# A second batch in mixed precision forms, and a planner with other costs

## The chip, the cores and the metric

The kernel runs on one core of a Trainium2 chip. The metric is the device time of one execution in microseconds (us). The programs of a core's engines run side by side and wait for each other by semaphores: TensorE (PE) multiplies matrices, VectorE (DVE) and ScalarE (ACT) work element by element, GpSimd (POOL) does the same kind of work, and SyncE (SP) issues all DMA transfers from one queue. Each engine takes its instructions strictly in the order of its program.

## The reference, cut to what matters

```
batch, n_heads, seq, head_dim = 4, 12, 448, 64
scores = where(causal, q @ k.T / sqrt(64), -1e9)       # per head, 448 x 448
attn   = softmax(scores)
x      = (attn @ v) -> 1792 tokens x 768               # heads side by side
g, val = x @ w_gate, x @ w_val                         # 768 -> 1536
out    = (g * sigmoid(g) * val) @ w_out                # 1536 -> 768
```

The weights arrive as 64-bit floats. All results have float32 precision.

## The kernel before, in words

**Tiling.** The four batches are four chunks of 448 tokens. For each chunk come the attention of 12 heads in pairs (heads 0 and 1, 2 and 3, ...) and then the gated layer ("MoE" in the code), which is computed transposed: 12 blocks of 128 hidden columns, each with a gate and a value product, then six output blocks. Attention of chunk c+1 is worked in between the matmuls of chunk c's gated layer.

**Two forms of a product.** TensorE takes a float32 product either in float32 itself, which costs four passes over the columns, or in the reduced format `float32r` with one pass. The gated layer splits each operand into a high part and a low part (`x = xh + xl`, `w = wh + wl`) and adds three one-pass products: lines 667, 668 and 669. Heads of a pair marked `'s'` (split) do the same: scores from `QS` and `KS` (line 431, three passes), values from `ph`, `pl` and `VS` (lines 551 and 553), where `VS` holds the high and the low part of V side by side, and the upper and lower halves of the result are added afterwards (`tmp`, line 561, and `xs`, line 562). Splitting costs element-wise work: `QS`, `KS` and `VS` twice each, `ph` and `pl` for each group of key blocks. Heads marked `'n'` multiply float32 directly: scores from `qraw` and `kraw`, values from `ph` and `vraw` (line 581). There each head has 64 rows or 64 columns of the array, so that the two heads of a pair share it; their values are multiplied for both heads in one step, and one copy (line 588) brings the pair's result to `xs`. Which form a pair takes is told by two lists, `NS` for the scores and `NP` for the values, with one entry a batch, read by `nat` (line 48): letter number `(h // 2) % len(entry)` holds for head `h`. Before, all pairs of batch 0 are `'n'` and all others `'s'`.

**The steps of a head.** Scores into PSUM (`S`); row maximum with the mask (line 453, VectorE); exponential (line 462, ScalarE); reciprocal of the sums (lines 473 and 474, VectorE); normalisation (lines 483, 487, 491, one of three engines); transposes by TensorE into `T` (line 512); copies `ph` of the transposed blocks (line 522), for split heads low parts (line 535); values into `O`; result to `xs`, split into `xh` and `xl` for the gated layer (lines 599 and 600). For split heads the first key block of 64 rows carries its high and low parts in one tile, so the VectorE operation for its low part writes `ph` as well (profile rows `ph<-T,ph`).

**The weights.** There are 36 groups of 128 x 768. In chunk 0 each is loaded as 64-bit pairs (`wide`), converted by one scaling and three bit operations on VectorE (`wraw`, lines 637, 641, 645), split into `whl` (lines 656 and 657) and stored in DRAM (`ws`, line 658). The later chunks load `ws` (line 622). So VectorE's weight work lies wholly in chunk 0.

**The order.** The order of all instructions is worked out before the run by `Planner.run` (line 93). Every operation has a due time, dependences, buffers that it takes, and for each engine that may do it a cost (`cost`, line 53). The planner goes through a modelled time: the engine takes, among the ready operations that can start at about the same moment, the one that is due first; where several engines may do an operation, the one that would end it first. `lock` models that GpSimd and some VectorE operations (`port`) exclude one another. The costs are nowhere used on the chip; they only set the order and which engine does what. On TensorE a change of kind (`t` for transposes against all other) adds `TURN`, a score step `TS`, a float32 value step `TV`.

Of the kernel before, what the change touches and what calls it, by code (L numbers as in the profile page):

```python
# [23 lines left out]
XD = [-10.0, 3.0]  # L24
CS = 0.0
UW = 0
NS = ['n', 's', 's', 's']
NP = ['n', 's', 's', 's']
LEN = [46.6, 112.0, 258.9, 133.6, 58.1]
FRAC = 0.96  # L30
FRAC0 = 0.6
# [3 lines left out]
BIAS = {'DVE': 1.3, 'ACT': 0.8, 'POOL': 0.8}  # L35
PVLATE = 0
LAT = {"PE": 0.29, "DVE": 0.2, "ACT": 0.23, "POOL": 0.2, "SP": 0.1}
TURN = 0.088
TS = 0.38
SG = [[[3, 0]], [[2, 1]]]  # L40
TV = 0.1
WINDOW = 96
KBUS = 1 / 320
DLAT = 1.8
# [38 lines left out]
class Planner:  # L83
# [9 lines left out]
    def run(self, caps):  # L93
        free = dict.fromkeys(("PE", "DVE", "ACT", "POOL", "SP"), 0.0)
        ring = {}
        lock = {"DVE": 0.0, "POOL": 0.0}
        wire = 0.0
        kind = None

        def begin(o, e, t):  # L100
            if e == "POOL":
                return max(t, lock["DVE"])
            if e == "DVE" and o.port:
                return max(t, lock["POOL"])
            return t

        def slots(tag):
            if tag not in ring:
                c = caps.get(tag.rstrip("0123456789"), 1)
                ring[tag] = [None] * c  # L110
            return ring[tag]

        avail = {e: [] for e in free}

        def push(o):
            for e in o.alts:
                avail[e].append(o)
            dirty.update(o.alts)

        def ready(o, e):  # L120
            t = 0.0
            for d in o.deps:
                x = d.end if d in o.soft else d.end + d.extra + (LAT[d.eng] if d.eng != e else (0.0 if e == "PE" else 0.13))
                if x > t:
                    t = x
            for i, r in enumerate(o.alloc):
                h = slots(r.tag)[sum(x.tag == r.tag for x in o.alloc[:i])]
                if h is not None:
                    if h.left:
                        return None  # L130
                    if h.end > t:
                        t = h.end
            return t

        def finish(o, e, s):
            best = s + o.alts[e][0] + BIAS.get(e, 0.0)
            for f in o.alts:
                if f != e:
                    r = ready(o, f)
                    if r is not None and begin(o, f, max(r, free[f])) + o.alts[f][0] + BIAS.get(f, 0.0) + 1e-6 < best:  # L140
                        return False
            return True

        def choose(e):
            lst = avail[e]
            lst.sort(key=lambda o: (o.due, o.idx))
            cand = []
            for o in lst[:WINDOW]:
                r = ready(o, e)
                if r is not None:  # L150
                    s = begin(o, e, max(r, free[e]))
                    if len(o.alts) == 1 or finish(o, e, s):
                        cand.append((s, o))
            if not cand:
                return None
            lim = max(min(s for s, _ in cand), free[e]) + DELTA[e]
            if e == "PE" and kind == "t":
                for s, o in cand:
                    if s <= lim and o.kind == "t":
                        return s, o  # L160
            for s, o in cand:
                if s <= lim:
                    return s, o
            return None

        dirty = set(free)
        for o in self.ops:
            if o.nd == 0:
                push(o)
        order = []  # L170
        left = len(self.ops)
        while left:
            best = None
            for e in free:
                c = choose(e)
                if c is not None and (best is None or (c[0], c[1].due) < (best[0], best[1].due)):
                    best = (c[0], c[1], e)
            assert best is not None
            s, o, e = best
            for f in o.alts:  # L180
                avail[f].remove(o)
            o.start, o.eng = s, e
            o.end = s + o.alts[e][0]
            if e == "PE":
                o.end += TURN * (o.kind == "t" != kind)
                kind = o.kind
            o.fn = o.alts[e][1]
            free[e] = o.end
            if e == "SP":
                wire = max(wire, o.end) + o.kb * KBUS  # L190
                o.extra = wire + DLAT - o.end
            if e == "POOL" or (e == "DVE" and o.port):
                lock[e] = o.end
            for r in o.alloc:
                q = slots(r.tag)
                q.pop(0)
                q.append(r)
            for r in o.uses:
                r.left -= 1
                r.end = max(r.end, o.end + o.extra + LAT[e])  # L200
            for d in o.outs:
                d.nd -= 1
                if d.nd == 0:
                    push(d)
            order.append(o)
            left -= 1
        return order
# [7 lines left out]
def kernel(  # L215
# [86 lines left out]
    def binary(n, out, a, b, alu=ALU.subtract, engines="DP", kind="two"):  # L302
        r = {}
        if "D" in engines:
            r["DVE"] = (cost("DVE", "two", n), lambda: nc.vector.tensor_tensor(out(), a(), b(), alu))  # L305
        if "P" in engines:
            r["port"] = True
            r["POOL"] = (cost("POOL", kind, n), lambda: nc.gpsimd.tensor_tensor(out(), a(), b(), alu))
        return r
# [294 lines left out]

    seq = [(c, g) for c in range(NCHUNK) for g in range(NW)]
    scratch = [dpool.tile([P, 2, WC], F32, tag=f"ws{g}", name=f"ws{g}") for g in range(NW)]
    wt, wops, stored = {}, {}, {}

    def weights(i):
        c, g = seq[i]  # L610
        due = start[c + 1] + LEN[c + 1] * g / NW
        w = wt[i] = {}
        rhl = Res("whl")

        def newhl():
            w["hl"] = buf([P, 2, WC], F32R, "whl", "whl", f"whl{i}")
            w["h"], w["l"] = w["hl"][:, 0], w["hl"][:, 1]

        if c:
            def load():  # L620
                newhl()
                nc.sync.dma_start(raw(w["hl"]), scratch[g])
            ld = op({"SP": (0.3, load), "kb": 768}, due - 10 * WLEAD, [stored[g]], [rhl])
            wops[i] = (ld, ld, rhl, rhl)
            return
        rw, r64 = Res("wraw"), Res("wide")

        def load():
            w["wide"] = buf([P, WC, 2], U32, "wide", "wide", f"wide{i}")
            nc.sync.dma_start(w["wide"], wP[g].bitcast(U32).rearrange("p (n w) -> p n w", w=2))  # L630
        ld = op({"SP": (0.3, load), "kb": 768}, due - 16 * WLEAD, alloc=[r64])
        hi = lambda: w["wide"][:, :, 1]
        hf = lambda: w["wide"].bitcast(F32)[:, :, 1]

        def shift():
            w["raw"] = buf([P, WC], F32, "wraw", "wraw", f"wraw{i}")
            nc.vector.tensor_scalar(w["raw"].bitcast(U32), hi(), 3, None, ALU.logical_shift_left)  # L637

        def sign():
            a = w["raw"].bitcast(U32)  # L640
            nc.vector.scalar_tensor_tensor(a, hi(), 0x80000000, a, ALU.bitwise_and, ALU.bitwise_or)  # L641

        def low():
            a = w["raw"].bitcast(U32)
            nc.vector.scalar_tensor_tensor(a, w["wide"][:, :, 0], 29, a, ALU.logical_shift_right, ALU.bitwise_or)  # L645

        dv = lambda kind, f: {"DVE": (cost("DVE", kind, WC), f), "port": True}
        g0 = op(copies("sbuf", WC, hf, hf, 2.0**-112), due - 10 * WLEAD, [ld], [], [r64])
        d0 = op(dv("one", shift), due - 9.5 * WLEAD, [g0], [rw], [r64])
        d1 = op(dv("two", sign), due - 9 * WLEAD, [d0], [], [r64, rw])  # L650
        ra = op(dv("two", low), due - 8.5 * WLEAD, [d1], [], [r64, rw])

        def newh():
            newhl()
            return w["h"]
        h = op(copies("sbuf", WC, newh, lambda: w["raw"]), due - 6 * WLEAD, [ra], [rhl], [rw])
        l = op(binary(WC, lambda: w["l"], lambda: w["raw"], lambda: raw(w["h"])), due - 5 * WLEAD, [h], [], [rw, rhl])
        stored[g] = op({"SP": (0.3, lambda: nc.sync.dma_start(scratch[g], raw(w["hl"]))), "kb": 768}, due - 3 * WLEAD,
                       [h, l], [], [rhl])
        wops[i] = (h, l, rhl, rhl)  # L660

    ps = {}

# [141 lines left out]
```

## Time and profile before

| | |
|---|---|
| median of three runs | 732.53 us (731.42 to 734.65) |
| the profiled execution, its span | 734.49 us, 732.7 us |
| busy: PE, DVE, ACT, POOL | 712.6, 395.5, 352.7, 220.8 us |
| instructions: PE, DVE, ACT, POOL | 3948, 921, 898, 256 |
| mean granted clock of TensorE | 0.991 |
| chain that ended last | PE 76%, DVE 14%, ACT 5%, DMA 3% |

Busy time counts the time in which an engine has at least one instruction running. In the rows below, PE is a matmul and PEld the load of its stationary operand. A float32 matmul has two records each. Times count from the first instruction of the profiled execution. A row that ends in brackets tells how long the engine was idle before it, and which engine's operation ended that.

### The profile page before, as it was taken

The numbers are of one execution on the slowest core, as the hardware profiler recorded it, in microseconds if no ns is written. First come the engines' busy times: TensorE is split into PE (matmuls) and PEld (weight loads), VectorE is DVE, ScalarE is ACT, GpSimd is POOL, SyncE is SP. The second block draws the span as 40 slices with busy tenths as digits, with TensorE's granted clock in tenths as the row PEclk, the third lists the DMA queues.
The fourth block names the chain that finished last, engine by engine and source line by source line (L and its number), as shares of the span: only waits on it lengthen the run. The fifth ranks groups of instructions, "written<-read, shape, count | busy, mean of one in ns | idle before, by whom it ended". The sixth has DMA issues, their size and how long they took to land.

```text
span 732.7 us, 10983 instructions
## 1 busy us (share of the span) xinstructions
PE 712.6 (97%) x3948; PEld 615.5 (84%) x3948; DVE 395.5 (54%) x921; ACT 352.7 (48%) x898; POOL 220.8 (30%) x256
## 2 busy tenths in 40 slices
PE   7999998999989999999999999999999999999997
PEld 3556987887878898898888988888888899999997
DVE  5888998999999455444453244554462222222100
ACT  6899466866847445345355253453462421111100
POOL 3686537564556142134222121231330000000000
PEclk9899999999999999999999999999999999999999
DMA  8787885887997865455565665644545566666671
GB/s 297 234 286 268 292 317 189 299 306 271 313 335 276 314 238 195 162 197 195 189 216 192 213 209 184 212 172 134 178 164 197 178 217 216 216 215 216 213 255 39
DMA packets 39798, 165.08 MB, mean 225 GB/s; under 512 B 4416, under 2 KB 13632, under 8 KB 39744
## 3 DMA queue, kind: packets, MB, share of 16 engines
q1 hardware_dynamic: 39744, 164.38, 64.3%
q8 instruction: 31, 0.51, 0.3%
q14 instruction: 23, 0.19, 0.1%
HBM read 130.55 MB, written 33.82 MB: 224 GB/s over the span
## 4 chain that ended last, share of the span: by engine, by line
PE 76%; DVE 14%; ACT 5%; DMA 3%; issue 1%; SPq 0%; ACTq 0%; DVEq 0%
PE M L667 13%; PE M L669 13%; PE M L668 13%; PE MO L667 7%; PE MO L669 7%; PE MO L668 7%; PE T L512 6%; PE S L431 5%; PE O L551 3%; DVE wraw L641 3%; DVE wraw L645 3%; DVE wraw L637 2%; ACT p L462 2%; PE O L553 2%; DVE whl L305 2%; DMA wide<-in_w_dram 2%
## 5 line engine op out<-in xcount | busy, mean ns | idle before, releaser
L667 PE MATMUL M<-xh,whl 128*128 128x448 f32 x576 | 217.1, 377 | 0.2 <-DVE t L703 0.2
L669 PE MATMUL M<-xh,whl 128*128 128x448 f32 x576 | 210.7, 366 | 0.0
L668 PE MATMUL M<-xl,whl 128*128 128x448 f32 x576 | 210.5, 365 | 0.0
L667 PEld LDWEIGHTS M<-xh,whl 128*128 128x128 f32 x576 | 108.3, 188 | 10.5 <-DVE t L703 0.5
L669 PEld LDWEIGHTS M<-xh,whl 128*128 128x128 f32 x576 | 108.2, 188 | 9.1
L668 PEld LDWEIGHTS M<-xl,whl 128*128 128x128 f32 x576 | 108.4, 188 | 8.1
L462 ACT ACTIVATE p<-p,m 64x64 f32<-64x64 f32 (+3 forms) x192 | 96.2, 506 | 37.9 <-DVE m L453 36.2
L667 PE MATMUL MO<-hh,whl 128*128 128x448 f32 x288 | 108.3, 376 | 0.0
L669 PE MATMUL MO<-hh,whl 128*128 128x448 f32 x288 | 105.8, 367 | 0.0
L668 PE MATMUL MO<-hl,whl 128*128 128x448 f32 x288 | 105.5, 366 | 0.0
L453 DVE CUSTOM_DVE_ANT_0 p<-S,mask 64x64 f32<-64x64 f32 (+1 forms) x192 | 70.6, 414 | 48.4 <-PE S L431 46.0
L283 ACT ACTIVATE ph<-T 64x448 fp32r<-64x448 f32 (+1 forms) x144 | 64.0, 503 | 44.3 <-PE T L512 42.8
L512 PE MATMUL T<-ident,p 128*128 128x128 f32 (+2 forms) x480 | 69.1, 280 | 1.2 <-POOL p L487 0.5
L512 PEld LDWEIGHTS T<-ident,p 128*128 128x128 f32 (+2 forms) x480 | 51.8, 132 | 21.3 <-issue 7.7
L703 DVE SCALAR_TENSOR_TENSOR t<-t,M 128x448 f32<-128x448 f32 x48 | 29.6, 617 | 64.5 <-ACT t L699 64.3
L283 ACT ACTIVATE hh<-t 128x448 fp32r<-128x448 f32 x38 | 21.9, 576 | 82.9 <-DVE t L709 82.9
L487 POOL TENSOR_SCALAR p<-p,rec 128x320 f32<-128x320 f32 (+3 forms) x77 | 45.0, 595 | 49.5 <-ACT p L462 30.1
L667 PEld LDWEIGHTS MO<-hh,whl 128*128 128x128 f32 x288 | 54.4, 189 | 4.7
L669 PEld LDWEIGHTS MO<-hh,whl 128*128 128x128 f32 x288 | 54.3, 189 | 4.7
L668 PEld LDWEIGHTS MO<-hl,whl 128*128 128x128 f32 x288 | 54.5, 189 | 4.2
L709 DVE TENSOR_TENSOR t<-t,M 128x448 f32<-128x448 f32 x48 | 29.6, 617 | 50.0 <-PE M L669 49.7
L699 ACT ACTIVATE t<-M 128x448 f32<-128x448 f32 x48 | 26.0, 542 | 59.9 <-PE M L669 58.4
(59 smaller groups left out, 911.1 us busy)
## 6 DMA issues: line engine op xcount, KB each, us to landing
whl<-ws SPq DMA_DIRECT2D x108, 768.0 KB, 4.3
wide<-in_w_dram SPq DMA_DIRECT2D x36, 768.0 KB, 6.0
ws<-whl SPq DMA_DIRECT2D x36, 768.0 KB, 4.5
vraw<-in_v_dram SPq DMA_DIRECT2D x24, 256.0 KB, 4.7
qraw<-in_q_dram SPq DMA_DIRECT2D x24, 224.0 KB, 4.0
kraw<-in_k_dram SPq DMA_DIRECT2D x24, 224.0 KB, 4.1
out_dram<-osb SPq DMA_DIRECT2D x24, 224.0 KB, 4.7
```

Source lines behind the costliest of these rows:

```text
L283: nc.scalar.activation(out(), in_(), AF.Copy, scale=scale)
L431: nc.tensor.matmul(st[u + y][f"S{i}"][: q1_ - q0], Q[:, q0:q1_], K[:, :q1_], start=z == 0, stop=z == len(passes) - 1)
L453: nc.vector.tensor_tensor_reduce(p[:r], s[f"S{i}"][:r], mask[:r, maskX - q0 : maskX - q0 + q1_], -0.125, 3.0e38, ALU.add, ALU.min, m[:r],)
L462: nc.scalar.activation(p[:r], p[:r], AF.Exp, bias=s[f"m{i}"][:r], scale=-1.0, accum_out=sums[u % NR][:r, i : i + 1],)
L487: nc.gpsimd.tensor_scalar(p[:r], p[:r], rec[u % NR][:r, i : i + 1], 0.0, ALU.mult, ALU.add)
L512: nc.tensor.transpose(pt[:kn, o_ + q0 - bs : o_ + q1_ - bs], s[f"p{i}"][:r, U.kb[j][0] : U.kb[j][1]], ident[:r, :r])
L667: nc.tensor.matmul(out[:, :n], a[:, w], xhi, start=first, stop=False)
L668: nc.tensor.matmul(out[:, :n], a[:, w], xlo, start=False, stop=False)
L669: nc.tensor.matmul(out[:, :n], l[:, w], xhi, start=False, stop=last)
L699: nc.scalar.activation(t, ps[c, f, 0][:, :N], AF.Tanh, scale=0.5)
L703: nc.vector.scalar_tensor_tensor(t, t, 1.0, ps[c, f, 0][:, :N], ALU.add, ALU.mult)
L709: nc.vector.tensor_tensor(t, t, ps[c, f, 1][:, :N], ALU.mult)
```

## The change

Batch 1's entry in both lists becomes `'ns'`: its pairs 0, 2 and 4 (heads 0, 1, 4, 5, 8, 9) take the float32 form, pairs 1, 3 and 5 stay split. The planner's costs change: a table of costs for each change of kind on TensorE (`m` gated layer and split values, `s` scores, `t` transposes, `v` float32 values), no extra time for score and value steps, and factors on what an operation takes in the plan: 1.25 for GpSimd, 1.12 for those VectorE operations that use the port shared with GpSimd. The third part lets weights be stored unsplit instead (`scratch1`, `RAW`); with `RAW = [0]` chunk 0 stores the split form and the later chunks load it, as before, so none of its new branches is taken.

```diff
-NS = ['n', 's', 's', 's']
-NP = ['n', 's', 's', 's']
+NS = ['n', 'ns', 's', 's']
+NP = ['n', 'ns', 's', 's']
-TURN = 0.088
-TS = 0.38
+TURN = {'ms': 0.19, 'sm': 0.19, 'mt': 0.09, 'tm': 0.085, 'ts': 0.19, ...}
+TS = 0.0
+PF = 1.12
+GF = 1.25
+RAW = [0]
-TV = 0.1
+TV = 0.0
...
-            o.end = s + o.alts[e][0]
+            o.end = s + o.alts[e][0] * (GF if e == "POOL" else PF if e == "DVE" and o.port else 1.0)
             if e == "PE":
-                o.end += TURN * (o.kind == "t" != kind)
+                o.end += TURN.get((kind or o.kind) + o.kind, 0.0)
...
+        if c and (g, "hl") in stored:
             def load():
                 newhl()
                 nc.sync.dma_start(raw(w["hl"]), scratch[g])
-            ld = op({"SP": (0.3, load), "kb": 768}, due - 10 * WLEAD, [stored[g]], [rhl])
+            ld = op({"SP": (0.3, load), "kb": 768}, due - 10 * WLEAD, [stored[g, "hl"]], [rhl])
             wops[i] = (ld, ld, rhl, rhl)
             return
...
+        h, l = split(ra, rw)
+        if 0 in RAW:
+            stored[g, "hl"] = keep(scratch[g], lambda: raw(w["hl"]), [h, l], rhl, 768)
```

All engines' programs are ordered anew. In the orders below a tile's first number is the head counted over all batches (`ph16` and `O16` belong to batch 1's head 4) or the weight group (`whl16`), and lines are those of each kernel: 305, 551, 553, 645, 667 to 669, 703 and 709 of before are 308, 554, 556, 672, 691 to 693, 727 and 733 after.

VectorE before, in the middle of batch 1's attention, around the first head of its third pair:

```order
L305 TENSOR_TENSOR whl16_1788<-wraw16_1631,whl16_1788 128x768
L645 SCALAR_TENSOR_TENSOR wraw17_1777<-wide17_1627,wraw17_1777 128x768
L637 TENSOR_SCALAR wraw18_1824<-wide18_1683 128x768
L305 TENSOR_TENSOR ph16_0_1810<-T16_0_1794,ph16_0_1810 64x448
L305 TENSOR_TENSOR pl16_1_1838<-T16_1_1800,ph16_1_1816 128x384
L305 TENSOR_TENSOR pl16_2_1842<-T16_2_1806,ph16_2_1822 128x384
L473 TENSOR_SCALAR rec1_77<-sums1_69 128x4
L474 RECIPROCAL rec1_77<-rec1_77 128x4
L703 SCALAR_TENSOR_TENSOR t0_7_1849<-t0_7_1849,M0_14_1779 128x448
L305 TENSOR_TENSOR xs2_86<-O16_1840,tmp16_1866 64x448
```

VectorE after, where the gated layer is at its blocks 14 to 16 as well:

```order
L668 SCALAR_TENSOR_TENSOR wraw18_1787<-wide18_1669,wraw18_1787 128x768
L308 TENSOR_TENSOR whl17_1805<-wraw17_1757,whl17_1805 128x768
L733 TENSOR_TENSOR t0_7_1796<-t0_7_1796,M0_15_1791 128x448
L672 SCALAR_TENSOR_TENSOR wraw18_1787<-wide18_1669,wraw18_1787 128x768
L664 TENSOR_SCALAR wraw19_1845<-wide19_1735 128x768
L308 TENSOR_TENSOR hl7_121<-t0_7_1796,hh7_109 128x448
L668 SCALAR_TENSOR_TENSOR wraw19_1845<-wide19_1735,wraw19_1845 128x768
L308 TENSOR_TENSOR whl18_1849<-wraw18_1787,whl18_1849 128x768
L672 SCALAR_TENSOR_TENSOR wraw19_1845<-wide19_1735,wraw19_1845 128x768
L727 SCALAR_TENSOR_TENSOR t0_8_1885<-t0_8_1885,M0_16_1827 128x448
```

The operations for `ph16`, `pl16` and `xs2` are gone from VectorE; weight operations and a low part of the hidden layer (`hl7`) follow each other there.

TensorE before, the values of the same head 16, between matmuls of the gated layer:

```order
L668 MATMUL M0_14_1779<-xl5_101,whl14_1629 128x448
L669 MATMUL M0_14_1779<-xh5_95,whl14_1629 128x448
L551 MATMUL O16_1840<-ph16_0_1810,VS16_1310 128x448
L667 MATMUL M0_15_1844<-xh0_90,whl15_1685 128x448
L668 MATMUL M0_15_1844<-xl0_96,whl15_1685 128x448
L669 MATMUL M0_15_1844<-xh0_90,whl15_1685 128x448
L551 MATMUL O16_1840<-ph16_1_1816,VS16_1310 128x384
L553 MATMUL O16_1840<-pl16_1_1838,VS16_1310 128x384
L551 MATMUL O16_1840<-ph16_2_1822,VS16_1310 128x256
L553 MATMUL O16_1840<-pl16_2_1842,VS16_1310 128x256
L551 MATMUL O16_1840<-ph16_2_1822,VS16_1310 128x128
L553 MATMUL O16_1840<-pl16_2_1842,VS16_1310 128x128
```

TensorE after, the values of heads 16 and 17 together:

```order
L692 MATMUL M0_17_1880<-xl3_99,whl17_1805 128x448
L693 MATMUL M0_17_1880<-xh3_93,whl17_1805 128x448
L584 MATMUL O17_1905<-ph16_0_1776,vraw16_1019 64x448
L584 MATMUL O17_1905<-ph17_0_1862,vraw16_1019 64x448
L584 MATMUL O17_1905<-ph16_1_1785,vraw16_1019 64x384
L584 MATMUL O17_1905<-ph17_1_1871,vraw16_1019 64x384
L584 MATMUL O17_1905<-ph16_2_1789,vraw16_1019 64x256
L584 MATMUL O17_1905<-ph17_2_1878,vraw16_1019 64x256
L584 MATMUL O17_1905<-ph16_2_1789,vraw16_1019 64x128
L584 MATMUL O17_1905<-ph17_2_1878,vraw16_1019 64x128
L691 MATMUL M0_17_1880<-xh4_94,whl17_1805 128x448
L692 MATMUL M0_17_1880<-xl4_100,whl17_1805 128x448
```

Both heads now stand in one run of eight matmuls, behind the transposes of head 17 and 18 matmuls of the gated layer.

TensorE before, from the last transposes of head 22 (batch 1's head 10, split in both kernels) to its first values:

```order
L512 MATMUL T22_2_2863<-ident_66,p22_3_2716 128x128 x2
L667 MATMUL MO0_4_2830<-hh3_105,whl32_2740 128x448
L668 MATMUL MO0_4_2830<-hl3_117,whl32_2740 128x448
L669 MATMUL MO0_4_2830<-hh3_105,whl32_2740 128x448
L667 MATMUL MO0_4_2830<-hh4_106,whl32_2740 128x448
L668 MATMUL MO0_4_2830<-hl4_118,whl32_2740 128x448
L669 MATMUL MO0_4_2830<-hh4_106,whl32_2740 128x448
L667 MATMUL MO0_4_2830<-hh5_107,whl32_2740 128x448
L668 MATMUL MO0_4_2830<-hl5_119,whl32_2740 128x448
L669 MATMUL MO0_4_2830<-hh5_107,whl32_2740 128x448
L551 MATMUL O22_2888<-ph22_0_2861,VS22_2420 128x448
```

TensorE after, the same place:

```order
L515 MATMUL T22_2_2765<-ident_66,p22_3_2621 128x128 x2
L691 MATMUL MO0_4_2721<-hh5_107,whl32_2626 128x448
L692 MATMUL MO0_4_2721<-hl5_119,whl32_2626 128x448
L693 MATMUL MO0_4_2721<-hh5_107,whl32_2626 128x448
L691 MATMUL MO0_4_2721<-hh6_108,whl33_2716 128x448
L692 MATMUL MO0_4_2721<-hl6_120,whl33_2716 128x448
L693 MATMUL MO0_4_2721<-hh6_108,whl33_2716 128x448
L554 MATMUL O22_2789<-ph22_0_2769,VS22_2045 128x448
```

Between the transposes and the values stand 9 matmuls of the gated layer before, and 6 after.

## Rows read from the trace of the kernel before

**Rows 1.** Windows, two stretches: length, busy time (instructions) of each engine, PEclk, DMA
```profile
60.00:246.00 186.00, 176.54 (x975) 151.70 (x975) 172.86 (x309) 125.90 (x287) 101.76 (x78) 0.98 0.78 284
246.00:590.00 344.00, 344.00 (x1982) 305.76 (x1982) 152.93 (x421) 156.23 (x418) 82.54 (x125) 1.00 0.57 195
```

**Rows 2.** Waits of PE, 46 to 250 us: total us, times, longest
```profile
PE O L551 <- DVE ph L305: 7.9, 6, 2.2
PE S L431 <- DVE m L453: 1.1, 4, 0.4
```

**Rows 3.** Timeline of PE, four such waits: start, us, operation, [idle before]
```profile
115.75 0.47 PE L551 MATMUL O<-ph,VS 128*128 128x448 f32 x1 [2.19 <-DVE ph L305]
...
139.60 0.47 PE L551 MATMUL O<-ph,VS 128*128 128x448 f32 x1 [0.48 <-DVE ph L305]
...
204.12 0.47 PE L551 MATMUL O<-ph,VS 128*128 128x448 f32 x1 [1.96 <-DVE ph L305]
...
235.89 0.47 PE L551 MATMUL O<-ph,VS 128*128 128x448 f32 x1 [1.06 <-DVE ph L305]
```

**Rows 4.** Timelines of DVE and PE: eighth and last weight groups, product and first use
```profile
80.59 1.49 DVE L305 TENSOR_TENSOR whl<-wraw,whl 128x768 fp32r<-128x768 f32 x1
...
95.06 0.37 PE L667 MATMUL M<-xh,whl 128*128 128x448 f32 x1
...
242.80 0.96 DVE L305 TENSOR_TENSOR whl<-wraw,whl 128x768 fp32r<-128x768 f32 x1
...
246.60 0.42 PE L667 MATMUL MO<-hh,whl 128*128 128x448 f32 x1
```

**Rows 5.** Timeline of PE: float32 sessions and pair, split head (to next row), split session
```profile
34.51 1.28 PE L431 MATMUL S<-kraw,qraw 64*128 64x448 f32 x8
...
36.20 1.13 PE L431 MATMUL S<-kraw,qraw 64*128 64x320 f32 x8
...
38.42 2.42 PE L581 MATMUL O<-ph,vraw 64*64 64x448 f32 x16
40.77 1.75 PE L431 MATMUL S<-kraw,qraw 64*128 64x448 f32 x8
...
123.37 0.54 PE L551 MATMUL O<-ph,VS 128*128 128x448 f32 x2
...
124.34 0.42 PE L667 MATMUL M<-xh,whl 128*128 128x448 f32 x1
...
251.64 1.02 PE L431 MATMUL S<-KS,QS 64*128 64x448 f32 x12
```

**Rows 6.** Groups of DVE by form: count, busy us, mean ns, idle before
```profile
L305 DVE TENSOR_TENSOR pl<-T,ph 128x384 fp32r<-128x384 f32 x72 | 36.8, 552 | 1.0
L305 DVE TENSOR_TENSOR whl<-wraw,whl 128x768 fp32r<-128x768 f32 x28 | 30.8, 1099 | 1.2 <-POOL whl L289 0.7 <-ACT whl L283 0.3
...
L305 DVE TENSOR_TENSOR hl<-t,hh 128x448 fp32r<-128x448 f32 x36 | 24.5, 682 | 19.3 <-ACT hh L283 16.4 <-POOL hh L289 2.9
...
L305 DVE TENSOR_TENSOR ph<-T,ph 64x448 fp32r<-64x448 f32 x36 | 22.2, 618 | 48.8 <-ACT ph L283 48.4
L305 DVE TENSOR_TENSOR xs<-O,tmp 64x448 f32<-64x448 f32 x36 | 22.2, 617 | 39.8 <-ACT tmp L283 39.5
...
L305 DVE TENSOR_TENSOR xl<-xs,xh 128x448 fp32r<-128x448 f32 x15 | 9.3, 623 | 3.8 <-ACT xh L283 3.2 <-POOL xh L289 0.5
```

**Rows 7.** Timelines of POOL and DVE at 112 us, two operations side by side
```profile
112.05 2.52 POOL L308 TENSOR_TENSOR whl<-wraw,whl 128x768 fp32r<-128x768 f32 x1
...
112.81 2.24 DVE L305 TENSOR_TENSOR hl<-t,hh 128x448 fp32r<-128x448 f32 x1
```

**Rows 8.** Windows, columns as in rows 1, two stretches with a lower clock
```profile
100.00:120.00 20.00, 17.40 (x92) 14.89 (x91) 18.78 (x34) 13.78 (x35) 10.26 (x8) 0.91 0.72 265
...
200.00:220.00 20.00, 18.04 (x97) 15.91 (x95) 18.51 (x24) 10.07 (x20) 10.73 (x7) 0.91 0.92 326
```

**Rows 9.** Windows, columns as in rows 1, end of batch 0's attention
```profile
40.00:60.00 20.00, 19.16 (x123) 10.98 (x120) 16.62 (x43) 20.00 (x62) 15.26 (x19) 1.00 0.88 296
```

More of the change, by code (lines that the diff above doesn't have):

```diff
@@ L37 @@
 LAT = {"PE": 0.29, "DVE": 0.2, "ACT": 0.23, "POOL": 0.2, "SP": 0.1}
-TURN = 0.088
-TS = 0.38
+TURN = {'ms': 0.19, 'sm': 0.19, 'mt': 0.09, 'tm': 0.085, 'ts': 0.19, 'st': 0.19, 'mv': 0.15, 'vm': 0.15, 'tv': 0.15, 'vt': 0.15, 'sv': 0.15, 'vs': 0.15}
+TS = 0.0
+PF = 1.12
+GF = 1.25
+RAW = [0]
 SG = [[[3, 0]], [[2, 1]]]
-TV = 0.1
+TV = 0.0
 WINDOW = 96
@@ L606 @@
     scratch = [dpool.tile([P, 2, WC], F32, tag=f"ws{g}", name=f"ws{g}") for g in range(NW)]
+    scratch1 = [dpool.tile([P, WC], F32, tag=f"wr{g}", name=f"wr{g}") for g in range(NW)]
     wt, wops, stored = {}, {}, {}
@@ L617, in newhl, with split, newh, keep @@
             w["h"], w["l"] = w["hl"][:, 0], w["hl"][:, 1]
-        if c:
+        def split(ra, rw):
+            def newh():
+                newhl()
+                return w["h"]
+            h = op(copies("sbuf", WC, newh, lambda: w["raw"]), due - 6 * WLEAD, [ra], [rhl], [rw])
+            l = op(binary(WC, lambda: w["l"], lambda: w["raw"], lambda: raw(w["h"])), due - 5 * WLEAD, [h], [], [rw, rhl])
+            wops[i] = (h, l, rhl, rhl)
+            return h, l
+        def keep(dst, src, deps, use, kb):
+            return op({"SP": (0.3, lambda: nc.sync.dma_start(dst, src())), "kb": kb}, due - 3 * WLEAD, deps, [], [use])
+        if c and (g, "hl") in stored:
             def load():
@@ L622, in load @@
                 nc.sync.dma_start(raw(w["hl"]), scratch[g])
-            ld = op({"SP": (0.3, load), "kb": 768}, due - 10 * WLEAD, [stored[g]], [rhl])
+            ld = op({"SP": (0.3, load), "kb": 768}, due - 10 * WLEAD, [stored[g, "hl"]], [rhl])
             wops[i] = (ld, ld, rhl, rhl)
+            return
+        if c:
+            rw = Res("wraw")
+            def load():
+                w["raw"] = buf([P, WC], F32, "wraw", "wraw", f"wraw{i}")
+                nc.sync.dma_start(w["raw"], scratch1[g])
+            ld = op({"SP": (0.3, load), "kb": 384}, due - 12 * WLEAD, [stored[g, "raw"]], [rw])
+            h, l = split(ld, rw)
+            if c in RAW and c < NCHUNK - 1:
+                stored[g, "hl"] = keep(scratch[g], lambda: raw(w["hl"]), [h, l], rhl, 768)
             return
@@ L651, in weights @@
         ra = op(dv("two", low), due - 8.5 * WLEAD, [d1], [], [r64, rw])
[L653 to L660, printed above, removed]
+        h, l = split(ra, rw)
+        if 0 in RAW:
+            stored[g, "hl"] = keep(scratch[g], lambda: raw(w["hl"]), [h, l], rhl, 768)
+        else:
+            stored[g, "raw"] = keep(scratch1[g], lambda: w["raw"], [ra], rw, 384)
     ps = {}
```

## The prediction

> **What bounds the kernel now.** I read the windows first. From 246 to 590 us TensorE is busy 344.00 of 344.00 us; there the time is its own work and nothing else can be won [rows 1]. From 60 to 246 us it is busy 176.54 of 186 us while VectorE is at 172.86, so two engines run there with almost no room, and only there can a change of VectorE's work be seen [rows 1]. Next, the waits of TensorE in that stretch: 7.9 us, in six waits, were ended by one operation, VectorE's `ph` (line 305), the low part of the first key block of a split head [rows 2]. The timeline places them: the first multiplication of a head's probabilities with V stands right behind its transposes, and VectorE has not got to that head yet [rows 3]. Last, the weights: the last product of a weight group starts on VectorE at 242.80 and takes 0.96 us, and TensorE first reads it at 246.60, under 3 us later [rows 4]. From there on TensorE does not wait. So the end of the run is 246.60 plus a rest that is fixed, and the question is when TensorE gets to that matmul: not before VectorE has unpacked 36 weight groups, and not before its own work and stalls are over.
>
> **What the change adds on TensorE.** Three pairs of the second batch (heads 0 and 1, 4 and 5, 8 and 9) take the form that the first batch has. Scores: the two sessions of a pair last 1.28 and 1.13 us in float32, and a split session 1.02, so 0.37 us more a pair. Values: a float32 pair takes 40.77 - 38.42 = 2.35 us, a split head 124.34 - 123.37 = 0.97 us, a pair 1.94; 0.41 us more [rows 5]. Three pairs: 3 x 0.78 = 2.3 us. The bounds: scores that cost no more give 3 x 0.41 = 1.2 us; every pair with one session at the 1.75 us that a row also shows (0.47 more than 1.28) gives 3.8 us [rows 5]. I take 2.3, as the other float32 sessions of batch 0 are nearer to the shorter rows. The transposes stay.
>
> **What it takes from VectorE.** A split pair costs VectorE two `ph` at 618 ns, four `pl` at 552 and two `xs` at 617: 4.68 us, three pairs 14.0 us [rows 6]. What replaces `xs` is one copy a pair, which in the new order stands on ScalarE. But the plan moves work back: before the last weight product, the new order has 11 `pl`, 6 `ph` and 6 `xs` fewer on VectorE (6.1 + 3.7 + 3.7 = 13.5 us), and five `xl` (623 ns), two `hl` (682) and one `whl` (1099) more: 5.6 us [rows 6]. Net 7.9 us of rows. Neighbouring operations overlap: I take a tenth off, 7.1 us of time. The weights could be ready at about 236.7 and not 243.8. GpSimd loses the splitting of Q, K and V of three pairs too. What that is worth shows at 112.05: a `whl` subtraction of 2.52 us runs on GpSimd, and beside it an `hl` on VectorE takes 2.24 us, where an `xl` of the same form has a mean of 623 ns [rows 6, 7]. Such a block lies right ahead of the longest wait, at 115.75 [rows 3]. I put nothing on this; the bounds are a loss of 3.1 us (both moved `hl` at 2.24 us and not 682 ns) and a gain of as much (two such blocks gone).
> [...]
>
> **What TensorE's waits do.** Of the 7.9 us, 0.48 and 1.96 (at 139.60 and 204.12) belong to heads that become float32; their `ph` is gone from VectorE, and in the new order both heads of such a pair are multiplied at once, at least 15 matmuls behind the second head's transposes: 2.4 us go. The other 5.5 us belong to heads that stay split. Their matmuls of cover between transposes and values change from 9 to 15 (the wait of 2.19 us), 12 to 9, 24 to 24 and 9 to 6 (the wait of 1.06 us). One has more room, two have less, and VectorE comes earlier by up to 7.1 us, with a plan that counts the operations that share GpSimd's port 12% longer. I let these fall by half, to 2.7 us, and the waits for the row maxima from 1.1 to 0.7 [rows 2]. So 9.0 us become 3.4: 5.6 us less; the bounds are 2.4 (nothing beyond the two heads) and 9.0.
> The granted clock is 0.91 in the stretches 100 to 120 and 200 to 220 us, that is 18% of each at 1.2 GHz instead of 2.4, worth 1.8 us each; both begin at one of the longest waits (115.75, 204.12) [rows 3, 8]. One of these waits goes with its `ph`, the other gets shorter; I count one drop gone, 1.8 us, with 0 to 3.6 as bounds.
>
> **The start.** From 40 to 60 us ScalarE is busy all the time [rows 9]. In the new order its copy of the last output of batch 0 stands two rows earlier, and a row took 20.00 / 62 = 0.32 us there: 0.7 us. VectorE gets to the early weights later, though: the operations ahead of the eighth group's last unpacking, each at the mean of its kind, are 74.6 us in the new order and 63.5 in the old, some 10 us of time. That group's product starts at 80.59 and takes 1.49 us, and it is first read at 95.06 [rows 4]: a slack of 13 us, of which 3 stay. I take a gain of 0.7 us, with a loss of 2 and a gain of 2 as bounds.
>
> **Sum**, against the profiled execution's own 734.49 us (span 732.7, 1.8 around it): +2.3 - 5.6 - 1.8 - 0.7 = -5.8, so 728.7 us there. The three runs shown have a median of 732.53, 2.0 under that execution; the forecast is 732.53 - 5.8 = **726.7 us**. VectorE allows it: TensorE would read the last weights at 240.8, VectorE has them at 236.7. Behind 246 us the order has the same work, and I count nothing.
>
> **Rivals.** *Both engines are set free.* VectorE's blocks at GpSimd go as well, all 9.0 us of waits and both clock drops vanish: 732.53 + 2.3 - 9.0 - 3.6 - 0.7 = 721.5 us. For it: 7.1 us of relief is nearly the whole of the `ph` waits. Against it: two split heads get 9 and 6 matmuls of cover, and five of the six waits stood behind 9 or 12.
> *The waits stay where heads stay split.* Only the 2.4 us go, and the float32 passes cost 2.3: 732.4 us, no change. For it: two of the four distances shrink. This is also the case in which relief of VectorE is relief of an engine that was not last.
> *Slower: TensorE runs into the shorter distances.* The values of heads 6 and 10 of the second batch stand 9 and 6 matmuls behind their transposes. A matmul is 0.2 us, so three fewer are 0.6 us more of waiting each; if they and head 2 wait 3.4 us each (2.19 + 1.2), that is 10.2 us in place of 7.9, a third clock drop adds 1.8, the float32 passes 2.3: 732.53 + 6.4 = 738.9 us. It decides once the `ph` waits stay above 6.0 us where neither clock nor start gives anything, above 8.5 where they give what I count. Against it: the plan with longer VectorE operations places these rows by a later `ph`, not an earlier one.
> That the change does not do what it says can be left out: the order shows 18 rows of `S<-kraw,qraw` of each width in place of 12.
>
> **How the numbers follow.** 0.58 for the forecast, which by the bounds of its terms lies between 722 and 731; 0.17 for both engines free; 0.15 for waits that stay; 0.10 for slower. A change under 0.5% (728.9 to 736.2) can't be told from none here. Faster: 0.48 + 0.17 + 0.02 = 0.67. Same: 0.10 + 0.13 + 0.02 = 0.25. Slower: 0.08. The range of 719 to 732.5 leaves out the slower rival and some of the no change.
>
> **What would show it.** In the profile after: the waits of TensorE for `ph` and the maxima between 46 and 250 us at 3.4 us and not 9.0, with at most one clock drop behind 60 us; VectorE's last `whl` near 237; TensorE's first reading of the last weight group near 241; sessions of float32 scores in the second batch at 1.1 to 1.3 us beside MoE matmuls. The forecast is wrong if the `ph` waits of the split heads keep their sum or grow, if TensorE waits for a weight group around 85 to 95 us, or if the float32 pairs cost more than 1.3 us each above the split ones.

## The result and the profile after

The changed kernel takes 720.89 us (median of 4 runs, 720.45 to 721.54), the kernel before 732.16 us (4 runs). The ratio is 0.984, with a 95% interval from 0.982 to 0.987. That is 11.3 us less where 5.8 were forecast: the direction and the place were right, the forecast gain was half of the measured one. The profiled execution took 721.01 us, its span is 719.0; against the one of before, which was 2.3 us above its median, the span is 13.7 us shorter.

Windows of the kernel after, columns as in [rows 1]; the last two rows are the stretches of [rows 8]:

```profile
60.00:246.00 186.00, 184.66 (x1030) 155.22 (x1026) 164.44 (x312) 132.85 (x302) 59.69 (x54) 1.00 0.87 321
246.00:580.00 334.00, 334.00 (x1917) 296.20 (x1916) 149.58 (x401) 154.01 (x408) 70.47 (x105) 1.00 0.56 189
...
100.00:120.00 20.00, 20.00 (x106) 16.87 (x105) 16.72 (x29) 12.69 (x25) 9.51 (x7) 1.00 0.82 284
200.00:220.00 20.00, 20.00 (x120) 16.22 (x119) 18.22 (x38) 15.17 (x37) 6.23 (x6) 1.00 1.00 404
```

TensorE is busy 184.66 of 186 us between 60 and 246 us and 176.54 before [rows 1], and both drops of the granted clock are gone. GpSimd is busy 59.69 us there, and was 101.76.

All waits of TensorE between 46 and 250 us after (total us, times, longest), for [rows 2]:

```profile
PE O L554 <- DVE ph L308: 1.1, 1, 1.1
PE T L515 <- ACT ph L286: 0.5, 1, 0.5
PE M L692 <- DVE xl L308: 0.2, 1, 0.2
```

One wait for `ph` is left of six. It is the one with 6 matmuls of cover, head 10 of batch 1, as the timeline of TensorE shows:

```profile
222.15 0.47 PE L554 MATMUL O<-ph,VS 128*128 128x448 f32 x1 [1.09 <-DVE ph L308]
```

The last product of the weights on VectorE, and TensorE's first matmul with it, and the first matmul with the eighth group (timelines, for [rows 4]):

```profile
92.80 0.37 PE L691 MATMUL M<-xh,whl 128*128 128x448 f32 x1
...
228.81 0.95 DVE L308 TENSOR_TENSOR whl<-wraw,whl 128x768 fp32r<-128x768 f32 x1
...
232.20 0.42 PE L691 MATMUL MO<-hh,whl 128*128 128x448 f32 x1
```

VectorE has the weights 14.0 us earlier than before, TensorE reads them 14.4 us earlier. The rest of the run, 486.8 us after and 486.1 before, is the same. So the whole gain lies ahead of that matmul, as forecast.

### The profile page after: what moved, and what is told of

It is laid out like the page before. It is cut to its first block, busy times and chain, and to the rows that moved or that the text cites. A ratio compares the mean times of both kernels' runs of the same rounds, so it can differ in the third digit from the quotient of the medians.

```text
span 719.0 us, 10894 instructions
## 1 busy us (share of the span) xinstructions
PE 707.0 (98%) x3930; PEld 604.9 (84%) x3930; DVE 378.2 (53%) x905; ACT 358.2 (50%) x907; POOL 163.3 (23%) x212
## 4 chain that ended last, share of the span: by engine, by line
PE 88%; ACT 6%; DVE 3%; POOL 1%; issue 1%; DMA 0%; SPq 0%; POOLq 0%; ACTq 0%
PE M L691 16%; PE M L692 16%; PE M L693 16%; PE MO L691 8%; PE MO L693 8%; PE MO L692 8%; PE T L515 6%; PE S L434 5%; ACT p L465 2%; PE O L554 2%; PE O L556 2%; ACT p L486 2%; ACT ph L286 1%; PE O L584 1%; POOL p L490 1%
## 5 line engine op out<-in xcount | busy, mean ns | idle before, releaser
L515 PE MATMUL T<-ident,p 128*128 128x128 f32 (+2 forms) x480 | 66.6, 273 | 2.9 <-ACT ph L286 2.6
L515 PEld LDWEIGHTS T<-ident,p 128*128 128x128 f32 (+2 forms) x480 | 49.5, 128 | 22.4 <-issue 9.3
L286 ACT ACTIVATE hh<-t 128x448 fp32r<-128x448 f32 x42 | 24.2, 576 | 81.3 <-DVE t L733 81.3
L486 ACT ACTIVATE p<-p,rec 128x448 f32<-128x448 f32 (+3 forms) x125 | 54.5, 500 | 3.2 <-DVE rec L477 2.2
```

Of the source, the lines that this page charges most:

```text
L286: nc.scalar.activation(out(), in_(), AF.Copy, scale=scale)
L486: nc.scalar.activation(p[:r], p[:r], AF.Copy, scale=rec[u % NR][:r, i : i + 1])
L515: nc.tensor.transpose(pt[:kn, o_ + q0 - bs : o_ + q1_ - bs], s[f"p{i}"][:r, U.kb[j][0] : U.kb[j][1]], ident[:r, :r])
```

## Experiments

All of them start from the changed kernel and undo or vary parts of it. A change of kind means that TensorE goes from one kind of matmul to another. Theory A: float32 heads relieve VectorE, and TensorE's waits go by that. Theory B: the plan's new lengths do it.

**The parts apart.** `heads_only` puts the old costs back, `plan_only` the old lists. `heads_port` has the heads and the two factors, `heads_turn` the heads and the table of changes of kind:

```diff
 heads_only:  -PF = 1.12  -GF = 1.25  +PF = 1.0  +GF = 1.0, old TURN, TS, TV
 plan_only:   -NS = ['n', 'ns', 's', 's']  +NS = ['n', 's', 's', 's'], NP the same
 heads_port:  old TURN, TS, TV; factors kept
 heads_turn:  -PF = 1.12  -GF = 1.25  +PF = 1.0  +GF = 1.0; new table kept
```

> Float32 heads in batch 1, the planner's costs as before. Theory A (relief of VectorE by the heads does it): TensorE's ph waits between 46 and 250 us fall below 3.5 us and the time to 723 to 726 us. Theory B (the plan's factors for shared-port operations do it, the heads are paid for by their passes): 730 to 733 us, with ph waits of 5 us or more and the granted clock still falling at 24 us.

> All of batch 1 split as before, all of the planner's new costs. Theory A: 729 to 733 us. Theory B: 721 to 725 us, the start (first gated-layer matmul) near 46 us and not 51, no drop of the clock at 24 us, and fewer ph waits though VectorE has all of its split work.

> Float32 heads and the factors 1.12 and 1.25, the costs for changes of kind on TensorE as before. If the factors matter and the table of changes does not: within 2 us of the changed kernel (720 to 723 us). If the table matters: 726 us or more.

> Float32 heads and the new table for changes of kind, factors 1.0. If the factors matter: 725 us or more, with blocks of VectorE by GpSimd and waits at ph as before. If the table matters: 720 to 723 us.

| kernel | median, us | ratio to before (95%) |
|---|---|---|
| heads only | 730.52 | 0.996 (0.994 to 0.997) |
| plan only | 732.86 | 1.000 (0.998 to 1.001) |
| heads and factors | 720.17 | 0.983 (0.981 to 0.985) |
| heads and table | 730.27 | 0.995 (0.994 to 0.997) |

Both theories fall as they were put. With the heads alone the waits for `ph` fall to 1.1 us, as theory A had it, but the time stays where theory B put it. With the plan alone the first gated-layer matmul starts at 47.83 us and not 51.05, and the clock drop at 24 us is gone (one comes at 41), nearly as theory B had it, but the time stays where theory A put it. The heads alone give 0.4%, the plan alone nothing, heads and factors the whole 1.7%; the table does nothing that can be told from noise (`heads_turn` waits 0.9 us for `ph`, and not as long as before, as was expected). Why shows at the last weight group. With the heads alone (VectorE, then TensorE):

```profile
229.73 0.95 DVE L308 TENSOR_TENSOR whl<-wraw,whl 128x768 fp32r<-128x768 f32 x1
...
242.96 0.42 PE L691 MATMUL MO<-hh,whl 128*128 128x448 f32 x1
```

VectorE is as early as in the changed kernel, but TensorE comes 12.3 us behind it. Its waits from 46 to 260 us are for other things now, spread over the attention (five of six rows):

```profile
PE S L434 <- DVE m L456: 2.7, 5, 1.1
PE T L515 <- ACT ph L286: 1.5, 1, 1.5
PE O L554 <- DVE ph L308: 1.1, 2, 0.7
PE M L691 <- ACT xh L286: 0.9, 1, 0.9
PE M L692 <- DVE xl L308: 0.8, 2, 0.5
```

With the plan alone it is the other way round, VectorE late and TensorE right behind it:

```profile
243.60 0.96 DVE L308 TENSOR_TENSOR whl<-wraw,whl 128x768 fp32r<-128x768 f32 x1
...
245.97 0.47 PE L691 MATMUL MO<-hh,whl 128*128 128x448 f32 x1
```

and TensorE waits for the weights themselves, which end none of its waits before (46 to 260 us, the first three rows):

```profile
PE MO L693 <- DVE whl L308: 2.8, 3, 1.2
PE T L515 <- ACT p L486: 2.5, 4, 1.1
PE M L693 <- DVE whl L308: 1.4, 2, 0.8
```

So two bounds lay on each other: VectorE's work, and the order of TensorE's program. Either one alone kept the run near its old time. A part of the order's share lies at the start. Windows of the first 60 us, with the heads alone and in the changed kernel:

```profile
0.00:60.00 60.00, 50.52 (x304) 28.27 (x304) 48.27 (x154) 51.17 (x160) 33.77 (x52) 0.97 0.75 259
```
```profile
0.00:60.00 60.00, 53.00 (x325) 29.15 (x327) 41.60 (x158) 54.09 (x169) 33.11 (x54) 1.00 0.70 243
```

TensorE is 2.5 us less busy there with the heads alone, and a clock drop takes 1.7 us more: about 4 of the 10 us that the factors give.

**Which factor.**

```diff
 heads_gf:  heads_port with  -PF = 1.12  +PF = 1.0
 heads_pf:  heads_port with  -GF = 1.25  +GF = 1.0
```

> Float32 heads, in the plan only GpSimd's factor 1.25 (VectorE's 1.0, old costs on TensorE). If the gain comes from GpSimd getting less work that blocks VectorE and from a better start: 720 to 724 us and the first gated-layer matmul by 48 us. If it comes from the plan knowing VectorE's own length: 728 to 731 us.

> Float32 heads, in the plan only VectorE's factor 1.12 for shared-port operations. If GpSimd's factor carries the gain: 727 to 731 us, first gated-layer matmul at 50 us or later. If VectorE's does: 720 to 724 us.

`heads_gf` takes 726.17 us, ratio 0.990 (0.988 to 0.991), and `heads_pf` 724.85 us, 0.988 (0.987 to 0.990): each gives about half of what both give. Of neither kernel does the time lie in a range that was expected (the first gated-layer matmul starts at 49.0 and 50.5 us); GpSimd's factor does not carry the gain by itself.

**Fit or luck.** Another order of some thousand instructions could be better by accident. `more` raises both factors, the `near` kernels change one of them by 2 to 4%; all have the heads and the old costs on TensorE.

```diff
 more:    +PF = 1.2    +GF = 1.4
 near_a:  +PF = 1.10   +GF = 1.25
 near_b:  +PF = 1.14   +GF = 1.25
 near_c:  +PF = 1.12   +GF = 1.20
 near_d:  +PF = 1.12   +GF = 1.30
```

> Float32 heads, old costs on TensorE, larger factors: 1.2 for VectorE's shared-port operations and 1.4 for GpSimd. If factors near the measured lengths are what matters, 1.12 and 1.25 are near enough and this is no better: 720 to 724 us. If any margin helps: 718 us or less.

> Float32 heads, old costs on TensorE, factors 1.10 and 1.25. Fit: 719 to 723 us. Luck of the order: anything from 719 to 730 us, the four of this call apart by 6 us or more.

> Factors 1.14 and 1.25. Fit: 719 to 723 us. Luck: as for the first of the four.

> Factors 1.12 and 1.20. Fit: 719 to 723 us. Luck: as for the first of the four.

> Factors 1.12 and 1.30. Fit: 719 to 723 us. Luck: as for the first of the four.

The four near ones take 720.52, 722.68, 723.06 and 722.80 us, ratios 0.983 to 0.987 with intervals of about 0.003 to either side: a band of 2.5 us (one of them 0.06 us above what was expected). With `heads_port` these are five orders between 720 and 723.1 us, so the gain is not the accident of one order. That the factors work because they fit what the engines measure is not shown: by `cost` a `whl` subtraction on VectorE counts 0.075 + 768/960 = 0.875 us, and before it has a mean of 1.10 us [rows 6] and a median of 0.95, so 1.26 and 1.09 times that; the 1.2 of `more` lies between them as 1.12 does. `more` takes 730.52 us (0.997, 0.996 to 0.998), outside what was expected of it. Its windows from 60 to 230 us show what is lost; first `more`, then `near_a`:

```profile
60.00:230.00 170.00, 164.44 (x901) 136.59 (x900) 148.05 (x277) 124.37 (x280) 51.75 (x46) 0.98 0.82 298
```
```profile
60.00:230.00 170.00, 168.89 (x942) 141.67 (x942) 155.79 (x284) 123.83 (x278) 55.61 (x51) 1.00 0.84 311
```

VectorE is busy 7.7 us less in `more`, though TensorE waits for its weights three times (136.7, 177.3 and 182.5 us), and one wait of TensorE for a normalisation on ScalarE, at 73.4 us, is 1.89 us long, with a clock drop behind it. So a kernel with larger factors is as slow as the one without any; with one such kernel, why is open.

**Is the early weight work what swallows the relief?** In `heads_only` VectorE has the last weight group ready 12.3 us ahead of its use and each other one 8 us or more, while TensorE waits for attention. The weights were given later due times:

```diff
 heads_late09:  heads_only with  -WLEAD = 1.2  +WLEAD = 0.9
 heads_late06:  heads_only with  -WLEAD = 1.2  +WLEAD = 0.6
```

> Float32 heads with the old plan costs, and the weight work due later (WLEAD 0.9 for 1.2). With the heads alone VectorE has the weights ready 9 to 17 us before TensorE reads them, and TensorE still waits for attention work. If that lead is what swallows the relief: 726 to 729 us, and a lead of 8 us or less. If the plan's wrong lengths are the cause and the lead only a sign: within 1.5 us of the heads alone (729 to 732 us).

> As before with WLEAD 0.6. If the lead swallows the relief: 724 to 728 us. If not: 729 us or more, and where weights come too late TensorE waits for them.

`heads_late09` takes 728.11 us (0.993, 0.992 to 0.994) and `heads_late06` 727.27 us (0.992, 0.991 to 0.993), against 0.996 for the heads alone. Both times lie in the first theory's range, and the lead at the last group is 11.5 us (not the 8 expected) and 7.0 us. Later weight work gives some 2 to 3 us of the 10 that the factors give. That the shorter lead is what gives them is not shown: with WLEAD 0.9 the lead at the last group is hardly shorter than the 12.3 us of `heads_only`, and with 0.6 the first gated-layer matmul also starts earlier, at 48.76 us and not 51.13.

**What a float32 pair costs, and how many are right.**

```diff
 b2ns:       NS, NP: -['n', 'ns', 's', 's']  +['n', 'ns', 'ns', 's']
 b1n:        NS, NP: -['n', 'ns', 's', 's']  +['n', 'n', 's', 's']
 two_pairs:  NS, NP: -['n', 'ns', 's', 's']  +['n', 'nss', 's', 's']
```

> The changed kernel with three pairs of batch 2 in float32 as well. Their attention runs where TensorE never waits, so this prices a float32 pair alone. Predicted price 0.78 us a pair: 2.3 us more than the changed kernel, 723.2 us (bounds 1.2 and 3.8). Rival: less work for the other engines pays there too, 720.9 us or less.

> All six pairs of batch 1 in float32, planner costs as changed. If TensorE's own work is the bound now, three more pairs cost 2.3 us and can win back at most the 1.8 us of waits that are left: 721 to 724 us, with the weights ready 8 us or more ahead of their first use. If VectorE still sets the arrival at the last weights (2.4 us ahead of TensorE there): 714 to 718 us.

> The changed kernel with two float32 pairs in batch 1 (0 and 3) and not three. TensorE saves about 1 us, VectorE has 4.7 us more to do, and it led by 2.4 us at the last weights. If VectorE takes over as the bound: 722 to 725 us. If TensorE stays the bound: 719.5 to 720.5 us.

`b2ns` takes 724.77 us, ratio 0.988 (0.987 to 0.990). Against the changed kernel's 0.984 this is 0.0039 x 732 = 2.9 us, 0.95 us a pair where 0.78 were worked out; the intervals of the two ratios still touch. The profiles have it closer. `b2ns` reads the last weight group of chunk 0 here:

```profile
232.91 0.42 PE L691 MATMUL MO<-hh,whl 128*128 128x448 f32 x1
```

From there to its end (span 722.4 us) are 489.4 us, in the changed kernel 486.8, and TensorE is busy 330.00 of the 330 us from 230 to 560: the three pairs cost 2.6 us, 0.86 each. `b1n` takes 721.95 us, 0.984 (0.983 to 0.986): no better, no worse. TensorE is its bound, as the last weight group shows, 14.6 us ahead of its use:

```profile
218.13 1.49 DVE L308 TENSOR_TENSOR whl<-wraw,whl 128x768 fp32r<-128x768 f32 x1 [1.01 <-POOL whl L292]
...
234.21 0.47 PE L691 MATMUL MO<-hh,whl 128*128 128x448 f32 x1
```

`two_pairs` takes 728.09 us with runs from 722.27 to 730.39, 0.992 (0.989 to 0.995). That is slower than either expectation. VectorE is last again; the waits of TensorE from 46 to 250 us begin with the weights:

```profile
PE MO L693 <- DVE whl L308: 3.8, 2, 2.4
PE M L693 <- DVE whl L308: 1.7, 1, 1.7
```

No version is clear of the changed kernel: heads and factors without the table, 0.983 (0.981 to 0.985), can't be told from it.

## Why the prediction was right and wrong

**Right.** The place of the bound (VectorE's weights and TensorE's waits for `ph` between 46 and 246 us), the direction, and that nothing changes behind the last weights. The passes were right too: 2.3 us forecast, 2.6 by the profile of `b2ns` and 2.9 by its median, inside 1.2 to 3.8; in batch 1 the score sessions of the changed kernel start at 115.40 and 123.20 us with 1.28 and 1.13 us, as in [rows 5].

**What failed.** Three terms of the sum were too small: the waits (5.6 us, measured 7.9), the clock (1.8 us, measured 6.8 in the profiled execution, 3.4 of it at a place that the sum did not look at), and behind the waits VectorE's relief (7.1 us, measured 14.0), largely because GpSimd's blocks of VectorE were put at nothing. And no term stood for the plan, without which the heads give 3 us.

**"I let these fall by half": the waits.** 9.0 us for `ph` and the maxima were to become 3.4; they became 1.1. VectorE was to be 7.1 us earlier at the last weights and is 14.0. Windows up to the end of that product, before and then after:

```profile
0.00:243.76 243.76, 227.34 (x1274) 179.90 (x1275) 217.97 (x461) 178.08 (x447) 138.22 (x131) 0.97 0.79 282
```
```profile
0.00:229.76 229.76, 221.42 (x1258) 170.00 (x1259) 199.23 (x445) 178.72 (x444) 87.67 (x100) 1.00 0.82 300
```

VectorE is busy 18.7 us less, and idle 4.7 us more. The part from the order, 7.9 us of rows in the forecast, is 6.4 by the groups of this stretch. Most of the rest is the next step.

**"I put nothing on this": GpSimd's blocks of VectorE.** The prediction priced such a block by `hl` alone, and over the whole run the mean of `hl` hardly changed: 668 ns after, 682 before [rows 6]. What got shorter are two others. Groups of VectorE up to the last weight product, before, after, and with the plan alone (count, busy us, mean ns, idle before):

```profile
L637 DVE TENSOR_SCALAR wraw<-wide 128x768 uint32<-128x768 uint32 x36 | 29.9, 834 | 1.2 <-ACT wide L283 1.2
L473 DVE TENSOR_SCALAR rec<-sums 128x4 f32<-128x4 f32 x24 | 11.1, 463 | 4.9 <-ACT p L462 4.8
```
```profile
L664 DVE TENSOR_SCALAR wraw<-wide 128x768 uint32<-128x768 uint32 x36 | 24.7, 686 | 3.1 <-ACT wide L286 2.9 <-POOL wide L292 0.2
L476 DVE TENSOR_SCALAR rec<-sums 128x4 f32<-128x4 f32 x24 | 5.6, 231 | 6.5 <-ACT p L465 6.4
```
```profile
L664 DVE TENSOR_SCALAR wraw<-wide 128x768 uint32<-128x768 uint32 x36 | 23.3, 654 | 0.0
L476 DVE TENSOR_SCALAR rec<-sums 128x4 f32<-128x4 f32 x24 | 5.9, 247 | 6.3 <-ACT p L465 6.2
```

5.2 and 5.5 us, 10.7 together: more than the 6.4 from the order. Both operations read one operand from SBUF. That GpSimd lengthens them shows in the rows of before up to 245 us. The 9 shifts (`wraw<-wide`) beside which GpSimd runs nothing have a mean of 0.55 us and none is longer, the 27 others one of 0.93; of `rec<-sums` 9 are alone, with 0.16 us, and 15 are not, with 0.65. The longest of these ends right ahead of the wait at 204.12 us [rows 3], beside this GpSimd operation (timelines of POOL and DVE):

```profile
201.06 2.12 POOL L308 TENSOR_TENSOR whl<-wraw,whl 128x768 fp32r<-128x768 f32 x1 [0.84 <-ACT whl L283]
...
201.43 1.78 DVE L473 TENSOR_SCALAR rec<-sums 128x4 f32<-128x4 f32 x1
```

But these lengths do not come with the heads: `heads_only` has 683 and 408 ns, and `plan_only`, with no head changed, 654 and 247. Either half takes work off GpSimd (busy 138.2 us up to VectorE's last weights before, 98.4 and 96.7 with one half, 87.7 with both). Nor do they decide the time alone. In `plan_only` the two bit operations that follow the shift take 82.4 us in place of 74.7, and VectorE subtracts 34 `whl` in place of 28, so it is no earlier; `heads_port`, as fast as the changed kernel and with VectorE's last product as early (228.76 us), has 703 and 379 ns. So what the blocks were worth by themselves is open: no run changed GpSimd's work alone.

**"I count one drop gone": the clock.** Both drops of [rows 8] went, 3.4 us and not 1.8. Windows put them here, before; half of the length is lost:

```profile
116.10:119.60 3.50, 3.50 (x17) 3.25 (x17) 2.87 (x6) 1.52 (x3) 0.80 (x1) 0.51 0.59 206
204.90:208.30 3.40, 3.40 (x13) 3.20 (x12) 3.14 (x5) 1.47 (x3) 2.08 (x2) 0.50 0.98 391
```

And a third drop was left out of the sum. Windows of 20 to 40 us, before and then after:

```profile
20.00:40.00 20.00, 18.76 (x108) 10.78 (x106) 16.81 (x56) 18.07 (x59) 14.19 (x20) 0.83 0.77 250
```
```profile
20.00:40.00 20.00, 17.89 (x121) 9.92 (x119) 15.69 (x58) 20.00 (x65) 11.21 (x17) 1.00 0.62 199
```

0.83 means a third of the stretch at 1.2 GHz, and 17% of 20 us is 3.4 us. It stood in the clock line of the first page. It begins at 24.0 us, behind TensorE's wait for a row maximum:

```profile
23.41 1.73 PE L431 MATMUL S<-kraw,qraw 64*128 64x448 f32 x6 [1.24 <-DVE m L453]
```

In the new order no wait there is longer than 1 us. The start was counted at 0.7 us; the eighth group's first matmul comes 95.06 - 92.80 = 2.3 us earlier, and most of what was won there is this drop, as TensorE's idle time ahead of that matmul hardly changed (7.5 us before, 7.2 after).

Not every execution has these drops. In the 45 executions of the kernel before that stand with the experiments, the mean granted clock lies between 0.990 and 0.998, most often at 0.995; the profiled one has 0.991. The ten with 0.992 or less take 734.6 us in the mean, the seven with 0.997 or more 732.3: 2.3 us apart, where the clock's share alone would be about 5. So the 6.8 us belong to the profiled execution, and less than that is in the medians.

**The rivals.** "Both engines are set free" came out, at 721.5 us, with a chance of 0.17; its waits and both clock drops went as it says. That the number is so near is in part luck: it has no term for the third drop, and takes the two drops of the profiled execution in full off a median in which they count for less. Against it the prediction set the 9 and 6 matmuls of cover. These were read as if VectorE's place in time were the old one; that the planner put the values there because VectorE was ahead is argued, no run tests it. The slower rival has no support: of the two places, the one with 9 has no wait, the one with 6 has 1.09 us.

**What the sum left out.** It treated the heads as the change and the plan as a side matter. The heads alone are worth 3 us, half of the forecast; with the factors it is 11 to 13. Nothing in the forecast's terms stood for that.

What was won ahead of the last weights, by windows up to TensorE's first matmul with them, before and then after:

```profile
0.00:246.60 246.60, 230.18 (x1291) 182.56 (x1291) 218.90 (x462) 178.08 (x447) 138.22 (x131) 0.97 0.79 283
```
```profile
0.00:232.20 232.20, 223.86 (x1273) 172.30 (x1273) 199.70 (x445) 178.72 (x444) 87.67 (x100) 1.00 0.82 300
```

Of the 14.4 us, 8.1 are idle time of TensorE (16.4 before, 8.3 after), nearly all of it the waits of 7.9. The other 6.3 are busy time: the three drops give 6.8, the passes take back 2.3 to 2.9, and 1.8 to 2.4 us are left, also in busy time, which no row here explains.

## What to carry to other kernels

Where two engines are both near full, relief of one can stay without effect until the order of the other changes too: undo each half of such a change before crediting either. The lengths in a planner are worth a trial of several values: here four pairs near 1.12 and 1.25 were all good, and none, as well as 1.2 and 1.4, were not. Read the clock line of the page for the whole span and price every drop, also in stretches that the change does not touch in name, and see from the clocks of other executions whether the drop is always there. Read what an operation costs from the stretch that is in question, and not from the mean of the whole run.

## What was not expected of the hardware

A `TENSOR_SCALAR` of 128 x 4 elements on VectorE took 0.16 us where GpSimd ran nothing beside it, and up to 1.78 us where it did; the reciprocal that follows it on the same elements took 178 ns in the mean: the small one with a scalar waits far longer for GpSimd than its size says. And waits can cost more than they last: both clock drops behind 60 us began right behind waits of 2.19 and 1.96 us [rows 3], and each took 1.7 us of TensorE's work. Not every such wait does it: `near_b` has one of 2.0 us and no drop.
